# Lone attention with two key chunks per tile and other small vector operations, and the first rank mix placed among batch 1's heads

## The chip, the cores and the metric

The kernel runs on one core of a Trainium2 chip. The metric is the device time of one execution in microseconds (us), as a median over runs. The engines are named as the profile does: PE is TensorE (PEld its weight loads), DVE is VectorE, ACT is ScalarE, POOL is GpSimd, and SP is SyncE, which issues nearly all DMAs here. Each engine works through its own queue of instructions in order. The source is written against a framework that fixes each engine's order when the kernel is built, with a timing model of its own; the order in which the source names things sets priorities, and only DMAs marked for it keep the source's order.

## The reference

Four batches of 448 tokens go through attention with 12 heads of 64, then through two mixers. All weights arrive as float64, and the kernel rebuilds float32 values from their bits.

```python
q_n, k_n = rmsnorm(q, g_q), rmsnorm(k, g_k)      # over the 64 of a head, eps 1e-6
attn = softmax(q_n @ k_n.T / 8)                  # sum + 1e-9
x = (attn @ v) as (B, S, 768)
# first mixer: rank 32 over the tokens, then 768 -> 3072 -> 768
u = x + (x.T @ U @ V).T
x = u + relu(u @ w_ch1) @ w_ch2
# second mixer: 448 -> 256 -> 448 over the tokens, then 768 -> 1536 -> 768
u = x + (relu(x.T @ w_tok1) @ w_tok2).T
out = u + relu(u @ w_ch1) @ w_ch2
```

## The kernel before, in words

Tokens are split into NC4 = 4 chunks of CP = 112. Most products run in float32r on a value split in a high part (ACT copy) and a low part (DVE or POOL subtraction), so that one float32 product becomes two or three.

**Attention** goes by pairs of heads. `load_pair` (L187) loads q, k, v, squares q on ACT (L204) and k with `mul` (L202; POOL's tensor_mul, DVE's for the very first pair), sums on DVE (L205), and forms 1/rms with small operations on 16 columns: L206 (mean and eps), Ln and Exp on ACT (L208, L209), one Newton step on DVE (L211 to L214). `turn_pair` (L233) transposes q and k on PE and rebuilds them, with DMAs on SP, as operands of a split product. `softmax` (L267) makes for each query chunk the scores in PSUM (`sc`), their negated maximum on DVE (L276), the exp on ACT (L278); after each second chunk DVE makes 1/(sum + 1e-9) (L281, L282) and POOL scales p (L285). `weigh` (L288) does for each key chunk `kc`: four PE transposes of p into a PSUM tile `pt` (L304), a copy to `ph` on ACT (L312), the rest `pl` on DVE (L316), and the products with v into `pv`. One head of each pair of batches 0 and 1 is `whole`: its products stay float32 (no `pl`). At the end `pv` goes into `xT` (L321, or L324 and L325).

`attention` (L327) is a generator: at step t it runs the softmax of head t + 1 beside the weighing of head t, chunk by chunk, turns the pair two ahead and loads the pair four ahead. Batches 0 and 1 (24 heads) run alone in the loop at L563; at step 8 U and V are loaded there (`load_uv`, L161). The loop breaks after t = 23. Then the first two w1 chunks are loaded, the PSUM and SBUF pools are closed and opened anew (L573 to L577), and the rank mix of batches 0 and 1 follows (L578). From L595 on, attention of batches 2 and 3 runs beside the first feed-forward layer of batches 0 and 1.

**Rank mix** (`rank_mix`, L392) does for each half of the channels: PE transposes back to tokens (`pt_x`, L372) with high and low parts on ACT (L379) and DVE (L380), products with U into `ps_h`, their copy `hst` (L404, L405), products with V into `ps_u`, and `split_u` (L384): DVE adds into xT (L385), ACT (L386) and POOL (L387) make `u`.

**Feed-forward** (`ffn`, L447) takes chunks of 128 hidden channels in groups of G = 2: `first` multiplies with a w1 chunk (`ps_g`, `gs`), `second` with a w2 chunk (`ps_x`) and adds to xT (L478). A weight chunk is loaded by `to_f32` (L111) into one of two raw buffers, rebuilt by ACT (L123, L128), DVE (L124, L125, L129) and POOL (L132), and split (L142 on ACT, L143 on POOL) into a destination from `slots` (L135), of which there are four high and four low. U takes one such pair of slots and V another, until the rank mixes have read them.

PSUM has eight banks. In lone attention: `s` (scores) three, `t` one, `p` four, and `pv` comes from `p` too. After the seam: `p` two, `v` one, `s` two, `t` one, `m` two.

Of the kernel before, what the change touches and what calls it, by code (L numbers as in the profile page):

```python
# [9 lines left out]
F32 = mybir.dt.float32  # L10
# [14 lines left out]
def attention_then_two_mixers(  # L25
# [28 lines left out]
    nc = tc.nc  # L54
# [8 lines left out]
    RC = T // P  # L63
    HALF = DM // 2
    G = 2
    PAIRS = ((0, 1), (2, 3))

    const = ctx.enter_context(tc.tile_pool(name="const", bufs=1))
    wp = ctx.enter_context(tc.tile_pool(name="wp", bufs=1))
# [19 lines left out]
    nc.vector.tensor_mul(gg, gq2, gk2)  # L89
    nc.vector.tensor_scalar_mul(gg, gg, 1.0 / D ** 0.5)  # L90

    def cols(x):
        return x.rearrange("r (c p) -> r c p", c=NC4)

# [1 line left out]
        return x.rearrange("r (p c) -> r c p", c=NC4)  # L96

    pools = {"late": False}
    AT = dict(qr=2, kr=2, vr=3, qn=1, vs=2, p=8, ph=3, pl=3, sq=1)

    def open_pools(stack, side):
        for nm, bufs, space in side:
# [84 lines left out]
    def load_pair(b, hp, whole, mul):  # L187
        h0 = 2 * hp
        raw = []
        for nm, src in (("q", q), ("k", k), ("v", v)):  # L190
            t = pools["at"].tile([CP, 2, NC4, D], F32, tag=f"{nm}r", bufs=AT[nm + "r"],
                        name=f"{nm}r")
            nc.sync.dma_start(t, src[b, h0:h0 + 2].rearrange("h (p c) d -> p h c d", c=NC4))
            raw.append(t)
        qr, kr, vr = raw

        ms = pools["at"].tile([CP, 2, 8], F32, tag="ms", name="ms")
        for i, t in enumerate((qr, kr)):
            sq = pools["at"].tile([CP, 2 * NC4, D], F32, tag="sq", bufs=AT["sq"], name="sq")
            tt = t.rearrange("p h c d -> p (h c) d")  # L200
            if i:
                mul(sq, tt, tt)  # L202
            else:
                nc.scalar.activation(sq, tt, AF.Square)  # L204
            nc.vector.reduce_sum(ms[:, i], sq, axis=AX.X)  # L205
        nc.vector.tensor_scalar(ms, ms, 1.0 / D, 1e-6, op0=ALU.mult, op1=ALU.add)  # L206
        rs = pools["at"].tile([CP, 2, 8], F32, tag="rs", name="rs")
        nc.scalar.activation(rs, ms, AF.Ln)  # L208
        nc.scalar.activation(rs, rs, AF.Exp, scale=-0.5)  # L209
        nt = pools["at"].tile([CP, 2, 8], F32, tag="nt", name="nt")  # L210
        nc.vector.tensor_mul(nt, rs, rs)  # L211
        nc.vector.tensor_mul(nt, nt, ms)
        nc.vector.tensor_scalar(nt, nt, -0.5, 1.5, op0=ALU.mult, op1=ALU.add)
        nc.vector.tensor_mul(rs, rs, nt)  # L214

        def scale(i, shape):
            return rs[:, i].rearrange("p (h c) -> p h c", h=2).unsqueeze(3).to_broadcast(shape)

        qn, kn = [], []
        for i, (nm, t, n) in enumerate((("qn", qr, qn), ("kn", kr, kn))):  # L220
            n.append(pools["at"].tile([CP, NC4, 2, D], F32, tag=nm, bufs=AT["qn"], name=nm))
            mul(
                n[0].rearrange("p c h d -> p h c d"), t, scale(i, [CP, 2, NC4, D]))
        qn, kn = qn[0], kn[0]

        vs = pools["at"].tile([CP, 2, NC4, 2, D], F32R, tag="vs", bufs=AT["vs"], name="vs")
        js = [j for j in range(2) if j not in whole]
        if js:
            js = slice(js[0], js[-1] + 1)
            split(vr[:, js], vs[:, js, :, 0], vs[:, js, :, 1])  # L230
        return qn, kn, [vr[:, j] if j in whole else vs[:, j] for j in range(2)]
# [35 lines left out]
    def softmax(pr, qs, ks, kt):  # L267
        for c in range(NC4):
            if c % 2 == 0:
                sm = pools["at"].tile([CP, 2], F32, tag="sm", bufs=6, name="sm")  # L270
            sc = psum("s", [CP, S], "sc")
            cs = slice(c * CP, (c + 1) * CP)
            mm(sc, qs[:, cs], ks, True, False)
            mm(sc, qs[:, cs], kt, False, True)
            nm = pools["at"].tile([CP, 1], F32, tag="nm", bufs=8, name="nm")
            nc.vector.tensor_reduce(nm, sc, axis=AX.X, op=ALU.max, negate=True)  # L276
            p = pools["pp"].tile([CP, S], F32, tag="p", bufs=AT["p"], name="p")
            nc.scalar.activation(p, sc, AF.Exp, bias=nm, accum_out=sm[:, c % 2:c % 2 + 1])  # L278
            pr.append(p)
            if c % 2:  # L280
                nc.vector.tensor_scalar_add(sm, sm, 1e-9)  # L281
                nc.vector.reciprocal(sm, sm)  # L282
                for i in range(2):
                    x = pr[c - 1 + i]
                    nc.gpsimd.tensor_scalar(x, x, sm[:, i:i + 1], 1.0, op0=ALU.mult, op1=ALU.mult)  # L285
            yield

    def weigh(pr, vj, j, dst, whole):  # L288

        pv = psum("v", [P, S], "pv")  # L290

        def product(kc, ph, pl):
            if whole:
                mm(pv[:D], vj[:, kc], ph, kc == 0, kc == NC4 - 1)
                return
            vk = vj[:, kc].rearrange("p t d -> p (t d)")
            mm(pv, vk, ph, kc == 0, False)
            mm(pv, vk, pl, False, kc == NC4 - 1)

        last = None  # L300
        for kc in range(NC4):
            pt = psum("p", [CP, S], "pt")
            for c in range(NC4):
                nc.tensor.transpose(  # L304
                    pt[:, c * CP:(c + 1) * CP], pr[c][:, kc * CP:(kc + 1) * CP],
                    ident[:CP, :CP],
                )
            if last:
                product(*last)
            ph = pools["pp"].tile([CP, S], F32 if whole else F32R, tag="ph", bufs=AT["ph"],  # L310
                                  name="ph")
            nc.scalar.activation(ph, pt, AF.Copy)  # L312
            pl = None
            if not whole:
                pl = pools["pp"].tile([CP, S], F32R, tag="pl", bufs=AT["pl"], name="pl")
                nc.vector.tensor_sub(pl, pt, f(ph))  # L316
            last = kc, ph, pl
            yield
        product(*last)
        if whole:  # L320
            nc.vector.tensor_copy(dst[j * D:(j + 1) * D], pv[:D])  # L321
            return
        tmp = pools["at"].tile([D, S], F32, tag="tmp", bufs=1, name="tmp")
        nc.scalar.activation(tmp, pv[D:], AF.Copy)  # L324
        nc.vector.tensor_add(dst[j * D:(j + 1) * D], pv[:D], tmp)  # L325
# [39 lines left out]


    def to_tokens(xT, hf):
        row = []
        for c in range(NC4):
            pt = psum("p", [CP, HALF], "pt_x")  # L370
            for i in range(3):
                nc.tensor.transpose(  # L372
                    pt[:, i * P:(i + 1) * P],
                    xT[:, 3 * hf + i, c * CP:(c + 1) * CP], ident,
                )
            s = (pools["xs"].tile([CP, 2, HALF], F32R, tag="xs", name="xs") if pools["xs"] is not pools["g"]
                 else pools["g"].tile([P, 2, S], F32R, tag="g", name="xs")[:CP, :, :HALF])
            hi, lo = s[:, 0], s[:, 1]
            nc.scalar.activation(hi, pt, AF.Copy)  # L379
            nc.vector.tensor_sub(lo, pt, f(hi))  # L380
            row.append((hi, lo))
        return row

    def split_u(xT, cc, pu, u):  # L384
        nc.vector.tensor_add(xT[:, cc], pu, xT[:, cc])  # L385
# [6 lines left out]
    def rank_mix(xT, uv):  # L392
# [1 line left out]
        u4, vh, vl = uv  # L394
        u = new_u()
        for hf in range(2):
            xs = to_tokens(xT, hf)
            ph = psum("t", [P, HALF], "ps_h")
            for c in range(NC4):
                for i in range(2):  # L400
                    mm(ph, u4[:, c].rearrange("p t r -> p (t r)"), xs[c][i],
                       c == 0 and i == 0, c == NC4 - 1 and i == 1)
            hst = pools["hs"].tile([P, HALF], F32R, tag="hs", name="hst")
            nc.scalar.activation(hst, ph, AF.Copy)  # L404
# [9 lines left out]
    def token_mix(xT, w):  # L414

        u = new_u()
        for hf in range(2):
            xs = to_tokens(xT, hf)
            ts = []
            for rc in range(RC):  # L420
                pt = psum("t", [P, HALF], "ps_t1")
# [124 lines left out]
    with ExitStack() as stack:  # L546
        open_pools(stack, (("hs", 1, 0), ("at", 2, 0)))
        inner = stack.enter_context(ExitStack())
        AT.update(p=12, ph=4, pl=4)
        open_pools(inner, (("pp", 1, 0), ("s", 3, 1), ("t", 1, 1), ("p", 4, 1)))  # L550
        pools["v"] = pools["p"]

        def new_xo():
            return pools["at"].tile([P, S], F32, tag="xo", bufs=1, name="xo")
# [8 lines left out]
        for t in att:  # L563
            if t == 8:
                pools["late"] = True
                uv = load_uv(False)
                pools["late"] = False
            if t == 2 * H - 1:
                break
        pools["late"] = True  # L570
        w1s = [w1_chunk(wa1, j) for j in range(G)]
        pools["late"] = False
        inner.close()  # L573
        AT.update(p=8, ph=3, pl=3)
        open_pools(stack, (("pp", 1, 0), ("g", 2 * G + 1, 0), ("p", 2, 1), ("v", 1, 1),
                           ("s", 2, 1), ("t", 1, 1), ("m", 2, 1)))
        pools["xs"] = pools["g"]  # L577
        for i in range(2):  # L578
            us[i] = rank_mix(xs[i], uv)


        def mix(i):
# [2 lines left out]
        def swap():  # L585
            for _ in att:
# [2 lines left out]
            open_pools(rest, (("wt", 1, 0), ("g", 2 * G, 0), ("xs", 8, 0), ("hs", 2, 0),  # L589
                              ("ts", 4, 0), ("ot", 2, 0), ("x3", 1, 0),  # L590
                              ("m", 3, 1), ("s", 2, 1), ("t", 1, 1), ("p", 2, 1)))
            wt.extend(load_wt())
            kept.extend(load_uv(True))

# [56 lines left out]
```

## Time and profile before

| | us |
|---|---|
| median of 3 runs | 1592.1 (1589.14 to 1592.72) |
| profiled execution, its own time | 1583.41 |
| profiled execution, span from first to last instruction | 1581.6 |
| lone attention, first score to last product | about 21 to 200.6 |
| seam with both rank mixes | about 200 to 241 |
| attention of batches 2 and 3 beside the first feed-forward layer | about 240 to 610 |

A row of the profile by line gives: line, engine, operation, out<-in with shapes and count, then busy time in us and mean ns of one, then the idle time just before and what ended it. A row of the timeline gives start, length, engine, line, operation and, in brackets, the idle time before it with its releaser. Spans are counted from the first instruction.

### The profile page before, as it was taken

How to read it: one execution, taken by the hardware profiler on the slowest of the kernel's cores; microseconds unless marked ns; L12 is line 12 of the kernel's file. 1: busy time of each engine (PE TensorE's matmuls, PEld its weight loads, DVE VectorE, ACT ScalarE, POOL GpSimd, SP SyncE). 2: the span in 40 equal slices, each digit the busy share in tenths (PEclk: the TensorE clock that was granted, in tenths of full speed). 3: DMA queues.
4: the chain of work that ended last, by engine and by line, in shares of the span. 5: the costliest groups of instructions: out<-in, count | busy, mean ns of one | idle time of the engine just before them, and what ended most of it. 6: DMA issues, size and time to landing. Idle time of an engine off the chain costs nothing.

```text
span 1581.6 us, 21878 instructions
## 1 busy us (share of the span) xinstructions
PE 1496.0 (95%) x7648; PEld 1303.0 (82%) x7648; DVE 1192.7 (75%) x1981; ACT 815.7 (52%) x1511; POOL 847.2 (54%) x645
## 2 busy tenths in 40 slices
PE   5999978999999999999999999999999999999998
PEld 3565566888788899898898988889999998998997
DVE  6899888988897887667858677677676676748663
ACT  5888765666566665434534345344344343524431
POOL 4667656666666554544745454455455453535540
PEclk9999979999999999999999999999999999999999
DMA  6656533445434422323314334233333332203312
GB/s 154 155 154 165 149 130 113 127 130 157 144 112 139 116 92 83 122 91 113 120 43 137 101 100 150 66 116 133 101 101 120 100 110 90 80 13 120 128 61 71
DMA packets 116046, 178.22 MB, mean 113 GB/s; under 512 B 9248, under 2 KB 105984, under 8 KB 115936
## 3 DMA queue, kind: packets, MB, share of 16 engines
q1 hardware_dynamic: 115616, 176.82, 36.7%
q8 instruction: 61, 1.00, 0.3%
q14 instruction: 49, 0.40, 0.1%
q10 hardware_dynamic: 320, 0.00, 0.0%
HBM read 135.50 MB, written 8.26 MB: 91 GB/s over the span
## 4 chain that ended last, share of the span: by engine, by line
PE 62%; DVE 12%; POOL 4%; DMA 4%; ACT 3%; issue 2%; SPq 0%; DVEq 0%; POOLq 0%; ACTq 0%
PE ps_x L77 27%; PE ps_g L77 25%; DVE w_bits L124 3%; DVE w_bits L129 2%; PE ps_u L77 2%; PE ps_t L77 2%; POOL w L143 2%; PE pv L77 2%; DMA qs<-hi 2%; DMA w_raw<-in_moe_w_ch_dram 1%; POOL w_bits L132 1%; DVE w_bits L125 1%; PE sc L77 1%; PE pt L304 1%; DVE xT L478 1%
## 5 line engine op out<-in xcount | busy, mean ns | idle before, releaser
L77 PE MATMUL ps_x<-gs,w 128*128 128x448 f32 x2592 | 566.5, 370 | 22.1 <-DVE xT L478 11.5
L77 PE MATMUL ps_g<-u,w 128*128 128x448 f32 x2592 | 546.4, 367 | 1.6 <-DVE gs L465 0.9
L77 PEld LDWEIGHTS ps_x<-gs,w 128*128 128x128 f32 x2592 | 483.4, 190 | 71.5 <-DVE xT L478 18.0
L77 PEld LDWEIGHTS ps_g<-u,w 128*128 128x128 f32 x2592 | 484.1, 188 | 42.2 <-DVE gs L465 1.5
L132 POOL TENSOR_TENSOR w_bits<-w_bits,w_round 128x768 uint32<-128x768 uint32 (+2 forms) x152 | 279.8, 1841 | 270.7 <-DVE w_bits L129 211.9
L143 POOL TENSOR_TENSOR w<-w_bits,w 128x768 fp32r<-128x768 f32 (+3 forms) x154 | 285.9, 1866 | 199.2 <-ACT w L142 198.9
L478 DVE TENSOR_TENSOR xT<-ps_x,xT 128x448 f32<-128x448 f32 x432 | 265.9, 619 | 121.4 <-PE ps_x L77 119.6
L128 ACT ACTIVATE w_round<-w_raw 128x768 uint32<-128x768 uint32 (+2 forms) x152 | 135.2, 889 | 186.2 <-POOL w_bits L132 186.0
L124 DVE TENSOR_SCALAR w_bits<-w_bits 128x768 f32<-128x768 f32 (+2 forms) x152 | 145.3, 956 | 96.0 <-ACT w_bits L123 95.9
L142 ACT ACTIVATE w<-w_bits 128x768 fp32r<-128x768 f32 (+3 forms) x154 | 124.8, 830 | 124.0 <-PE ps_x L77 68.0
L285 POOL TENSOR_SCALAR p<-p,sm 112x448 f32<-112x448 f32 x192 | 129.0, 685 | 95.3 <-DVE sm L282 49.0
L123 ACT ACTIVATE w_bits<-w_raw 128x768 f32<-128x768 f32 (+2 forms) x152 | 135.3, 891 | 85.5 <-POOL w L143 77.7
L129 DVE SCALAR_TENSOR_TENSOR w_bits<-w_raw,w_bits 128x768 uint32<-128x768 uint32 (+2 forms) x152 | 168.7, 1110 | 2.1
L278 ACT ACTIVATE p<-sc,nm 112x448 f32<-112x448 f32 x192 | 121.9, 637 | 49.8 <-DVE nm L276 41.9
L125 DVE TENSOR_SCALAR w_bits<-w_bits 128x768 uint32<-128x768 uint32 (+2 forms) x152 | 137.7, 906 | 2.9
L464 ACT ACTIVATE gs<-ps_g 128x448 fp32r<-128x448 f32 x144 | 77.8, 543 | 108.8 <-PE ps_g L77 106.1
L465 DVE SCALAR_TENSOR_TENSOR gs<-ps_g,gs 128x448 fp32r<-128x448 f32 x144 | 88.9, 619 | 52.8 <-ACT gs L464 52.5
L276 DVE TENSOR_REDUCE nm<-sc 112x1 f32<-112x448 f32 x192 | 116.3, 613 | 8.4 <-PE sc L77 7.8
L304 PEld LDWEIGHTS pt<-ident,p 112*112 112x112 f32 x768 | 86.7, 134 | 41.5 <-issue 18.5
L312 ACT ACTIVATE ph<-pt 112x448 fp32r<-112x448 f32 (+1 forms) x192 | 101.3, 546 | 30.2 <-PE pt L304 29.0
L304 PE MATMUL pt<-ident,p 112*112 112x112 f32 x768 | 111.4, 262 | 5.2 <-DVE pl L316 2.6
L387 POOL TENSOR_TENSOR u<-xT,u 128x448 fp32r<-128x448 f32 x48 | 59.1, 1248 | 65.5 <-ACT u L386 65.5
(74 smaller groups left out, 1438.4 us busy)
## 6 DMA issues: line engine op xcount, KB each, us to landing
w_raw<-in_moe_w_ch_dram SPq DMA_DIRECT2D x144, 768.0 KB, 4.4
ks<-hi SPq DMA_DIRECT2D x96, 112.0 KB, 2.4
kt<-lo SPq DMA_DIRECT2D x96, 112.0 KB, 2.3
qr<-in_q_dram SPq DMA_DIRECT2D x24, 224.0 KB, 3.1
kr<-in_k_dram SPq DMA_DIRECT2D x24, 224.0 KB, 3.2
vr<-in_v_dram SPq DMA_DIRECT2D x24, 224.0 KB, 3.1
qs<-hi SPq DMA_DIRECT2D x48, 112.0 KB, 2.8
qs<-lo SPq DMA_DIRECT2D x48, 112.0 KB, 2.7
```

The source lines that it names most:

```text
L77: nc.tensor.matmul(o, lhsT=l, rhs=r, start=start, stop=stop)
L123: nc.scalar.activation(f(w), f(high), AF.Abs)
L124: nc.vector.tensor_scalar_max(f(w), f(w), TINY)
L125: nc.vector.tensor_scalar(w, w, 3, 0x3FFFFFF8, op0=ALU.logical_shift_left, op1=ALU.bitwise_and)
L128: nc.scalar.activation(r, low, AF.Copy, scale=2.0 ** -29)
L129: nc.vector.scalar_tensor_tensor(w, high, 0xC0000000, w, op0=ALU.bitwise_and, op1=ALU.bitwise_or)
L132: nc.gpsimd.tensor_tensor(w, w, r, op=ALU.add)
L142: nc.scalar.activation(hi, w, AF.Copy)
L143: nc.gpsimd.tensor_sub(lo, w, f(hi))
L285: nc.gpsimd.tensor_scalar(x, x, sm[:, i:i + 1], 1.0, op0=ALU.mult, op1=ALU.mult)
L304: nc.tensor.transpose(pt[:, c * CP:(c + 1) * CP], pr[c][:, kc * CP:(kc + 1) * CP], ident[:CP, :CP],)
L478: nc.vector.tensor_add(xT[:, dc], px, xT[:, dc])
```

## The change

- In lone attention `weigh` takes two key chunks per tile (`AT["turn"]` = 2): `pt` becomes a tile of two banks, with one ACT copy and one DVE subtraction over both chunks. Later attention keeps one chunk per tile.
- PSUM in lone attention: `s` two banks, `t` one, `p` two tiles of two banks, `pv` one bank of its own. `ph` and `pl` have two buffers of double size.
- The square of q uses `mul` (POOL, or DVE for the first pair), as that of k, in all attention.
- Four kinds of small DVE operation on 2 or 16 columns become scalar_tensor_tensor, two of them with a constant tile (`eps`, `zeros`) as second input; the Newton step has three operations in place of four.
- `rank_mix` of batch 0 is called at step t = 13 of the loop of lone attention, with its `xs` tiles in the buffers of `ph`. `rank_mix` of batch 1 stays behind the loop. `to_tokens` is a generator.

```diff
-    AT = dict(qr=2, kr=2, vr=3, qn=1, vs=2, p=8, ph=3, pl=3, sq=1)
+    AT = dict(qr=2, kr=2, vr=3, qn=1, vs=2, p=8, ph=3, pl=3, sq=1, turn=1)
...
-            if i:
-                mul(sq, tt, tt)
-            else:
-                nc.scalar.activation(sq, tt, AF.Square)
+            mul(sq, tt, tt)
             nc.vector.reduce_sum(ms[:, i], sq, axis=AX.X)
-        nc.vector.tensor_scalar(ms, ms, 1.0 / D, 1e-6, op0=ALU.mult, op1=ALU.add)
+        nc.vector.scalar_tensor_tensor(
+            ms, ms, 1.0 / D, eps[:CP], op0=ALU.mult, op1=ALU.add)
...
-        nc.vector.tensor_mul(nt, rs, rs)
+        nc.vector.scalar_tensor_tensor(nt, rs, -0.5, rs, op0=ALU.mult, op1=ALU.mult)
         nc.vector.tensor_mul(nt, nt, ms)
-        nc.vector.tensor_scalar(nt, nt, -0.5, 1.5, op0=ALU.mult, op1=ALU.add)
-        nc.vector.tensor_mul(rs, rs, nt)
+        nc.vector.scalar_tensor_tensor(rs, nt, 1.5, rs, op0=ALU.add, op1=ALU.mult)
...
-                nc.vector.tensor_scalar_add(sm, sm, 1e-9)
+                nc.vector.scalar_tensor_tensor(
+                    sm, sm, 1e-9, zeros[:CP], op0=ALU.add, op1=ALU.add)
...
-        for kc in range(NC4):
-            pt = psum("p", [CP, S], "pt")
-            for c in range(NC4):
-                nc.tensor.transpose(
-                    pt[:, c * CP:(c + 1) * CP], pr[c][:, kc * CP:(kc + 1) * CP],
-                    ident[:CP, :CP],
-                )
+        n = AT["turn"]
+        for k0 in range(0, NC4, n):
+            kcs = range(k0, k0 + n)
+            pt = psum("p", [CP, n, BANK], "pt")[:, :, :S]
+            for i, kc in enumerate(kcs):
+                for c in range(NC4):
+                    nc.tensor.transpose(
+                        pt[:, i, c * CP:(c + 1) * CP], pr[c][:, kc * CP:(kc + 1) * CP],
+                        ident[:CP, :CP],
+                    )
             if last:
                 product(*last)
...
-                pl = pools["pp"].tile([CP, S], F32R, tag="pl", bufs=AT["pl"], name="pl")
+                pl = pools["pp"].tile([CP, n, S], F32R, tag="pl", bufs=AT["pl"], name="pl")
                 nc.vector.tensor_sub(pl, pt, f(ph))
-            last = kc, ph, pl
-            yield
+            last = kcs, ph, pl
+            for _ in kcs:
+                yield
...
-        AT.update(p=12, ph=4, pl=4)
-        open_pools(inner, (("pp", 1, 0), ("s", 3, 1), ("t", 1, 1), ("p", 4, 1)))
-        pools["v"] = pools["p"]
+        AT.update(p=12, ph=2, pl=2, turn=2)
+        open_pools(inner, (("pp", 1, 0), ("s", 2, 1), ("t", 1, 1), ("p", 2, 1), ("v", 1, 1)))
...
+            if t == H + 1:
+                pools["new_xs"] = lambda: pools["pp"].tile(
+                    [CP, 2, S], F32R, tag="ph", bufs=AT["ph"], name="xs")
+                us[0] = rank_mix(xs[0], uv)
             if t == 2 * H - 1:
                 break
...
-        for i in range(2):
-            us[i] = rank_mix(xs[i], uv)
+        pools["new_xs"] = lambda: pools["g"].tile([P, 2, S], F32R, tag="g", name="xs")
+        us[1] = rank_mix(xs[1], uv)
```

## Rows read from the trace of the kernel before

**Rows 1.** Busy time of the engines, share of the span, instructions.
```profile
PE 1496.0 (95%) x7648; PEld 1303.0 (82%) x7648; DVE 1192.7 (75%) x1981; ACT 815.7 (52%) x1511; POOL 847.2 (54%) x645
```

**Rows 2.** Stages: length, busy of each engine (instructions), PE's granted clock, DMA share, GB/s.
```profile
25.00:200.00 175.00, 164.09 (x862) 101.67 (x861) 157.44 (x389) 142.48 (x381) 112.32 (x151) 0.99 0.63 160
200.00:241.00 41.00, 33.12 (x150) 27.70 (x149) 32.96 (x49) 27.16 (x49) 26.28 (x18) 0.79 0.32 105
241.00:248.00 7.00, 0.77 (x5) 0.32 (x3) 7.00 (x4) 1.67 (x5) 5.22 (x5) 0.86 0.12 33
```

**Rows 3.** Timeline of the seam, engine by engine: start, length, instruction, idle before.
```profile
200.18 0.47 PE L77 MATMUL pv<-pl,vs 112*128 112x448 f32 x1
...
203.75 0.69 PE L77 MATMUL ps_h<-xs,w 112*128 112x384 f32 x1 [3.10 <-ACT xs L379]
...
237.12 0.68 PE L77 MATMUL ps_x<-gs,w 128*128 128x448 f32 x2 [1.41 <-ACT w L142]
...
239.63 0.62 DVE L385 TENSOR_TENSOR xT<-ps_u,xT 128x448 f32<-128x448 f32 x1 [0.24 <-PE ps_u L77]
240.31 6.32 DVE L124 TENSOR_SCALAR w_bits<-w_bits 128x768 f32<-128x768 f32 x1
...
236.20 0.86 ACT L142 ACTIVATE w<-w_bits 128x768 fp32r<-128x768 f32 x1
...
216.61 1.83 POOL L132 TENSOR_TENSOR w_bits<-w_bits,w_round 128x768 uint32<-128x768 uint32 x1 [0.96 <-DVE w_bits L129]
```

**Rows 4.** Rank mixes: pieces of the chain (start, length), then groups from 188 to 241.
```profile
221.85 1.24 PE ps_g L77 x6
...
223.89 0.35 PE ps_h L77 x2
...
225.65 0.33 PE pt_x L372 x3
...
232.34 0.83 PE ps_u L77 x4
...
L387 POOL TENSOR_TENSOR u<-xT,u 128x448 fp32r<-128x448 f32 x9 | 10.8, 1223 | 5.4 <-ACT u L386 5.4
...
L380 DVE TENSOR_TENSOR xs<-pt_x,xs 112x384 fp32r<-112x384 f32 x16 | 8.5, 551 | 2.7 <-ACT xs L379 2.5
...
L385 DVE TENSOR_TENSOR xT<-ps_u,xT 128x448 f32<-128x448 f32 x12 | 7.1, 617 | 2.7 <-PE ps_u L77 2.7
```

**Rows 5.** Groups by line and shape in lone attention, 25 to 200 us.
```profile
L276 DVE TENSOR_REDUCE nm<-sc 112x1 f32<-112x448 f32 x93 | 56.1, 613 | 3.8 <-PE sc L77 3.5
...
L205 DVE TENSOR_REDUCE ms<-sq 112x8 f32<-112x512 f32 x28 | 18.8, 673 | 2.8 <-POOL sq L202 1.6 <-ACT sq L204 1.2
...
L202 POOL TENSOR_TENSOR sq<-kr 112x512 f32<-112x512 f32 x14 | 14.7, 1050 | 6.9 <-DMA kr<-in_k_dram 3.3 <-DVE ms L205 1.5 <-DVE sm L281 1.4
```

**Rows 6.** Small operations: duration min/median/max in ns over the run; one stall's timeline.
```profile
L206 DVE TENSOR_SCALAR ms<-ms x24: 148/172/4299, 8.9 to 456.7; 112x16 f32<-112x16 f32 x24
...
L213 DVE TENSOR_SCALAR nt<-nt x24: 148/175/3693, 12.0 to 461.5; 112x16 f32<-112x16 f32 x24
...
L214 DVE TENSOR_TENSOR rs<-rs,nt x24: 148/174/1740, 12.2 to 463.1; 112x16 f32<-112x16 f32 x24
...
273.25 3.69 DVE L213 TENSOR_SCALAR nt<-nt 112x16 f32<-112x16 f32 x1
...
273.29 1.84 POOL L132 TENSOR_TENSOR w_bits<-w_bits,w_round 128x768 uint32<-128x768 uint32 x1
275.09 1.82 POOL L143 TENSOR_TENSOR w<-w_bits,w 128x768 fp32r<-128x768 f32 x1
...
278.53 0.59 PE L304 MATMUL pt<-ident,p 112*112 112x112 f32 x4 [2.62 <-DVE pl L316]
```

**Rows 7.** The scores `sc` from 25 to 200 us: one group, one wait (us, times).
```profile
L278 ACT ACTIVATE p<-sc,nm x94: 617/635/694, 25.3 to 187.1; 112x448 f32<-112x448 f32 x94
...
  ACT p L278: 9.6, 21
```

More of the change, by code (lines that the diff above doesn't have):

```diff
@@ L65, in attention_then_two_mixers @@
     G = 2
-    PAIRS = ((0, 1), (2, 3))
+    BANK = 512
     const = ctx.enter_context(tc.tile_pool(name="const", bufs=1))
@@ L90, in attention_then_two_mixers @@
     nc.vector.tensor_scalar_mul(gg, gg, 1.0 / D ** 0.5)
+    zeros = const.tile([P, 2], F32, name="zeros")
+    nc.vector.memset(zeros, 0.0)
+    eps = const.tile([P, 16], F32, name="eps")
+    nc.vector.memset(eps, 1e-6)
     def cols(x):
@@ L200, in load_pair @@
             tt = t.rearrange("p h c d -> p (h c) d")
-            if i:
-                mul(sq, tt, tt)
-            else:
-                nc.scalar.activation(sq, tt, AF.Square)
+            mul(sq, tt, tt)
             nc.vector.reduce_sum(ms[:, i], sq, axis=AX.X)
-        nc.vector.tensor_scalar(ms, ms, 1.0 / D, 1e-6, op0=ALU.mult, op1=ALU.add)
-        rs = pools["at"].tile([CP, 2, 8], F32, tag="rs", name="rs")
+        ms = ms.rearrange("p a b -> p (a b)")
+        nc.vector.scalar_tensor_tensor(
+            ms, ms, 1.0 / D, eps[:CP], op0=ALU.mult, op1=ALU.add)
+        rs = pools["at"].tile([CP, 16], F32, tag="rs", name="rs")
         nc.scalar.activation(rs, ms, AF.Ln)
         nc.scalar.activation(rs, rs, AF.Exp, scale=-0.5)
-        nt = pools["at"].tile([CP, 2, 8], F32, tag="nt", name="nt")
-        nc.vector.tensor_mul(nt, rs, rs)
+        nt = pools["at"].tile([CP, 16], F32, tag="nt", name="nt")
+        nc.vector.scalar_tensor_tensor(nt, rs, -0.5, rs, op0=ALU.mult, op1=ALU.mult)
         nc.vector.tensor_mul(nt, nt, ms)
-        nc.vector.tensor_scalar(nt, nt, -0.5, 1.5, op0=ALU.mult, op1=ALU.add)
-        nc.vector.tensor_mul(rs, rs, nt)
+        nc.vector.scalar_tensor_tensor(rs, nt, 1.5, rs, op0=ALU.add, op1=ALU.mult)
+        rs = rs.rearrange("p (a b) -> p a b", a=2)
         def scale(i, shape):
@@ L290, in weigh, with product @@
         pv = psum("v", [P, S], "pv")
[L292 to L298, printed above, removed]
-        last = None
-        for kc in range(NC4):
-            pt = psum("p", [CP, S], "pt")
-            for c in range(NC4):
-                nc.tensor.transpose(
-                    pt[:, c * CP:(c + 1) * CP], pr[c][:, kc * CP:(kc + 1) * CP],
-                    ident[:CP, :CP],
-                )
+        def product(kcs, ph, pl):
+            for i, kc in enumerate(kcs):
+                if whole:
+                    mm(pv[:D], vj[:, kc], ph[:, i], kc == 0, kc == NC4 - 1)
+                    continue
+                vk = vj[:, kc].rearrange("p t d -> p (t d)")
+                mm(pv, vk, ph[:, i], kc == 0, False)
+                mm(pv, vk, pl[:, i], False, kc == NC4 - 1)
+        last = None
+        n = AT["turn"]
+        for k0 in range(0, NC4, n):
+            kcs = range(k0, k0 + n)
+            pt = psum("p", [CP, n, BANK], "pt")[:, :, :S]
+            for i, kc in enumerate(kcs):
+                for c in range(NC4):
[3 more added lines that the diff above has]
+                    )
             if last:
                 product(*last)
-            ph = pools["pp"].tile([CP, S], F32 if whole else F32R, tag="ph", bufs=AT["ph"],
+            ph = pools["pp"].tile([CP, n, S], F32 if whole else F32R, tag="ph", bufs=AT["ph"],
                                   name="ph")
@@ L367, in to_tokens @@
     def to_tokens(xT, hf):
-        row = []
         for c in range(NC4):
@@ L375, in to_tokens @@
                 )
-            s = (pools["xs"].tile([CP, 2, HALF], F32R, tag="xs", name="xs") if pools["xs"] is not pools["g"]
-                 else pools["g"].tile([P, 2, S], F32R, tag="g", name="xs")[:CP, :, :HALF])
+            s = pools["new_xs"]()[:CP, :, :HALF]
             hi, lo = s[:, 0], s[:, 1]
@@ L380, in to_tokens @@
             nc.vector.tensor_sub(lo, pt, f(hi))
-            row.append((hi, lo))
-        return row
+            yield hi, lo
     def split_u(xT, cc, pu, u):
@@ L396, in rank_mix @@
         for hf in range(2):
-            xs = to_tokens(xT, hf)
             ph = psum("t", [P, HALF], "ps_h")
-            for c in range(NC4):
+            for c, xs in enumerate(to_tokens(xT, hf)):
                 for i in range(2):
-                    mm(ph, u4[:, c].rearrange("p t r -> p (t r)"), xs[c][i],
+                    mm(ph, u4[:, c].rearrange("p t r -> p (t r)"), xs[i],
                        c == 0 and i == 0, c == NC4 - 1 and i == 1)
@@ L417, in token_mix @@
         for hf in range(2):
-            xs = to_tokens(xT, hf)
+            xs = list(to_tokens(xT, hf))
             ts = []
@@ L573, in attention_then_two_mixers @@
         inner.close()
-        AT.update(p=8, ph=3, pl=3)
+        AT.update(p=8, ph=3, pl=3, turn=1)
         open_pools(stack, (("pp", 1, 0), ("g", 2 * G + 1, 0), ("p", 2, 1), ("v", 1, 1),
                            ("s", 2, 1), ("t", 1, 1), ("m", 2, 1)))
-        pools["xs"] = pools["g"]
-        for i in range(2):
-            us[i] = rank_mix(xs[i], uv)
+        pools["new_xs"] = lambda: pools["g"].tile([P, 2, S], F32R, tag="g", name="xs")
+        us[1] = rank_mix(xs[1], uv)
         def mix(i):
@@ L591, in swap @@
                               ("m", 3, 1), ("s", 2, 1), ("t", 1, 1), ("p", 2, 1)))
+            pools["new_xs"] = lambda: pools["xs"].tile([P, 2, HALF], F32R, tag="xs", name="xs")
             wt.extend(load_wt())
```

## The prediction

> **What bounds the kernel now.** I read the page's busy line first: TensorE is busy 95% of the span, VectorE 75% [rows 1]. So only time in which TensorE is kept waiting can be won. The table by stage tells where that is [rows 2]. From 460 us on (the pure feed-forward layers) nothing is touched. From 25 to 200 us attention of batches 0 and 1 runs alone: TensorE 164.09 of 175 us (94%) and VectorE 157.44 (90%), so two engines are near full there and work added to either costs about its own length. From 200 to 241 us, the seam between lone attention and the first feed-forward layer, TensorE shows 33.12 of 41 us, part of it at a granted clock of 0.79 on average (below the 2.4 GHz level); and from 241 to 248 us it does 0.77 of 7 us.
>
> The timeline of the seam shows why [rows 3]. The last product of lone attention starts at 200.18; the first rank-mix product at 203.75; the last addition of the two rank mixes is at 239.63. The first ps_x product, with which the second half of the first feed-forward group begins, is at 237.12 and waited for ACT's split of a w2 chunk (L142, 236.20). Those integer weights were ready at 216.61 + 1.83 = 218.4 us. What held the split was its destination: `slots()` has four buffers, U and V hold two until both rank mixes are over, and the two w1 chunks hold the others. So the path through the seam is: end of attention, rank mix 0, rank mix 1, U's slots free, w2 split, ps_x.
>
> **The change part by part.** 1. *Batch 0's rank mix leaves the seam.* The two mixes take 203.75 to 240.25 = 36.5 us, 18 us each, paced by the ACT, VectorE, TensorE relay and the weight chain between. With one left, U comes free some 18 us sooner. Batch 0's `u` exists already, so its ps_g products (36 in [rows 2]'s second stage, at a pure step of about 0.205 us, 1.24 us for six [rows 4], 7.4 us) can run beside mix 1 (7.9 us of TensorE, below): 15.3 of 18 us, so TensorE has room. Next late is the w2 chunk itself: ready 18 us after the end of attention (200.6 to 218.4), just when mix 1 would end (3 + 18 = 21 us after). So the weights take the rest of the gain at most in part: I take -16 us. Bounds: -18 if the mix is the only limit; -8 if the weight chain (four chunks through ACT, VectorE, POOL and two raw buffers) sets the pace.
>
> 2. *The same mix among batch 1's heads.* It issues no DMA; load_uv stays at t = 8, so SP's queue is not crossed. TensorE pieces at full clock [rows 4]: eight groups of three transposes at 0.33 us, 2.6; sixteen ps_h at 0.35 for two, 2.8; twelve ps_u at 0.83 for four, 2.5: 7.9 us. VectorE: 8 x 0.551 + 6 x 0.617 + 2 x 0.56 (two hst subtractions, taken as long as an xs one) = 9.2 us. POOL: six u subtractions at 1.223, 7.3 us, ahead of the p products (L285) that the transposes wait for. At 94% and 90% busy I charge +8 us. Bounds: +3 if the 11 us that TensorE lacks to 175 take half of it, +13 if VectorE's 9.2 us and the sharing of `ph`'s two buffers (xs uses them, and the heads' ph waits behind) add up.
>
> 3. *Two key chunks per tile.* One VectorE subtraction of 896 columns in place of two. L205 with 512 columns takes 673 ns, L276 with 448 takes 613 [rows 5]: 60 ns for 64 columns, so some 0.19 us of each instruction is fixed. Part of it overlaps with the neighbours; 24 merged pairs save at most 4.6 us of VectorE. ACT saves a like amount on 48 pairs, and the squares. TensorE saves nothing. As TensorE is as full as VectorE, I take -2 us (0 to -5).
>
> 4. *Square of q on POOL* in place of ACT: 24 x 1.05 us [rows 5], 12.6 of them in the 175 us where POOL is busy 112.32 [rows 2]. What waits behind it are the p products. Cover: POOL's idle third. +1 us (0 to +4). Head 0's square goes to VectorE, 0.69 us at most at the start, in these bounds.
>
> 5. *Other forms of the small operations.* VectorE's tensor_scalar on 16 columns (L206, L213) has a median of 172 to 175 ns, but maxima of 4.30 and 3.69 us; the two-tensor form L214, as small, stays at 1.74 at most [rows 6]. The long one at 273.25 ends as POOL's second instruction in a row (273.29, 275.09) does: a tensor_scalar waited through a hand-over between POOL instructions. The two-input forms waited too, but for one instruction (the longest there is 1.84 us). So scalar_tensor_tensor with a tile as second input should cap the wait at one POOL instruction, not remove it: of 3.69 + 4.30 us at most 1.84 each would be left, so 4.3 us or more of VectorE goes. TensorE lost 2.62 us at the first [rows 6]. I take -3 us (0 to -7), and the small operation that goes is in it.
>
> By the Trainium skill, page "SBUF — State Buffer", section "Who interferes with whom", a VectorE instruction with two SBUF inputs contends with a GpSimd instruction that reads SBUF just as a two-port mode does, and the second to start blocks fully. By that rule alone part 5 is 0 and the sum 3 us higher. The trace agrees that both forms wait; it does not show them waiting equally long.
>
> 6. *PSUM is dealt anew*: scores get two banks for three, pt two double banks, pv one bank of its own. This adds waits: with three banks score products already waited 21 times for exp, 9.6 us [rows 7]. Behind a waiting score on TensorE's queue stand transposes and products of the current head. Also pv of a head now waits for the last one's L325. +2 us; bounds 0 (pt's four chunks cover it) and +15 (next section).
>
> 7. *The 6.32 us wait of L124* at 240.31 [rows 3], which empties TensorE from 241 to 248, keeps its form. POOL's queue of u subtractions and splits ahead of it is halved, so it may go (-6) or come back elsewhere (0); I take 0.
>
> Sum: -16 + 8 - 2 + 1 - 3 + 2 + 0 = -10 us. The profiled execution took 1583.4 us (span 1581.6); it would come to about 1573. The median of the three timed runs is 1592.1, 0.55% above it, so I put the difference on the median: 1582.
>
> **The rivals.** A. *The score ring of two becomes the bound of lone attention (slower).* From starts and ends of the 94 scores of that stage [rows 7], a bank is held 3.7 us from product to end of exp on average, so three banks hold 1.96 at a time; with two there is no slack. 70 of 94 products began within 0.2 us of, or before, the end of the exp two chunks earlier, by 67 us in all. Against it: the holding time is mostly queueing (0.4 us product, 0.53 reduction, 0.55 exp, under 2 us with hand-overs) and shrinks when fewer are in flight. If a fifth of the 67 us comes back as waiting on TensorE, that is 13 us where I took 2: the sum is +1, and a third of it, 22 us, gives +10. It decides from 12 us, 0.5 us a head. Time 1593 to 1602.
>
> B. *The weights set the pace of the seam.* Then part 1 is -8 and the sum -2: 1590. For it: four chunks pass at about 6 us each (POOL's L132 of the third at 216.61). Against it: w2's chunk stood ready for 18 us.
>
> C. *The mix hides in lone attention and the L124 wait goes*: +3 and -6, giving -21: 1571.
>
> D. *The new forms change nothing* (both wait one POOL instruction or several alike): sum -7, 1585. The page named above states this rule.
>
> **How the numbers follow.** Two tenths of a per cent, 3.2 us, is about what a measurement of this kernel can tell from no change. Chances: forecast 0.40 (own range 1577 to 1588), D 0.10, C 0.13, B 0.15, A 0.22. Faster by over 0.2%: forecast, D, C and a little of B, 0.65. Same: most of B and the mild end of A, 0.14. Slower: the rest of A and of B, 0.21. The range goes from C's 1571 to within A, 1598, leaving out under 2 in 10.
>
> **What would show it.** Right: the last addition of the rank mix (L385) some 18 us after the end of lone attention, not 39; first ps_x about 20 us after it, not 36.5; lone attention ending 5 to 9 us later; no small scalar_tensor_tensor over 2 us. Wrong: waits of sc for exp in lone attention well over 9.6 us (A); the split L142 of w2 waiting for POOL's L132 and not for the rank mix (B); L281, L206 at 4 us again (D).

## The result and the profile after

The changed kernel took 1603.83 us (median of four runs, 1602.32 to 1605.74) against 1590.8 us before (median of four runs, the three known before and one more): ratio 1.0082, 95% interval 1.0062 to 1.0102. It is 13 us slower where 10 us faster was forecast. The profiled execution took 1602.33 us, its span 1600.5 us. That is 18.9 us more than the profiled execution of before, whose 1583.41 us lie under all of its timed runs; differences between stages, below, are between profiled executions.

The busy line, then the stages of the changed kernel (columns as in [rows 1] and [rows 2]): lone attention, the seam, and the stretch of lone attention that holds batch 0's rank mix.

```profile
PE 1501.5 (94%) x7648; PEld 1310.9 (82%) x7648; DVE 1192.5 (75%) x1936; ACT 798.9 (50%) x1439; POOL 870.1 (54%) x668
...
25.00:235.00 210.00, 180.27 (x910) 113.90 (x909) 164.69 (x361) 138.57 (x333) 130.33 (x169) 0.98 0.53 132
235.00:266.00 31.00, 21.33 (x94) 18.20 (x94) 24.34 (x34) 18.81 (x33) 20.09 (x13) 0.78 0.35 115
142.00:160.00 18.00, 15.91 (x82) 10.74 (x82) 11.42 (x25) 10.88 (x24) 7.35 (x8) 1.00 0.16 36
```

The engines' work is about what it was. Lone attention is 35 us longer (210 us where [rows 2] had 175), and its two busiest engines are further from full: TensorE 86%, VectorE 78%. The seam is shorter. So in lone attention engines wait for one another more than before. The timeline of the seam, engine by engine, as in [rows 3]:

```profile
234.78 0.37 PE L77 MATMUL pv<-pl,vs 112*128 112x448 f32 x1
238.47 0.69 PE L77 MATMUL ps_h<-xs,w 112*128 112x384 f32 x1 [3.32 <-ACT xs L388]
242.96 1.01 PE L77 MATMUL ps_h<-xs,w 112*128 112x384 f32 x2 [3.81 <-DVE xs L389]
...
247.19 3.65 PE L77 MATMUL ps_g<-u,w 128*128 128x448 f32 x16
...
251.64 3.96 PE L77 MATMUL ps_g<-u,w 128*128 128x448 f32 x18
...
259.34 1.04 PE L77 MATMUL ps_h<-xs,w 112*128 112x384 f32 x2 [1.12 <-ACT xs L388]
...
263.94 0.96 PE L77 MATMUL ps_x<-gs,w 128*128 128x448 f32 x2
...
238.19 3.00 DVE L218 SCALAR_TENSOR_TENSOR rs<-nt,rs 112x16 f32<-112x16 f32 x1
...
242.35 1.02 DVE L389 TENSOR_TENSOR xs<-pt_x,xs 112x384 fp32r<-112x384 f32 x2
...
265.61 0.61 DVE L393 TENSOR_TENSOR xT<-ps_u,xT 128x448 f32<-128x448 f32 x1
...
260.86 0.87 ACT L147 ACTIVATE w<-w_bits 128x768 fp32r<-128x768 f32 x1
...
237.41 1.99 POOL L148 TENSOR_TENSOR vs<-vr,vs 112x512 fp32r<-112x512 f32 x1 [8.00 <-ACT vs L147]
239.37 1.79 POOL L137 TENSOR_TENSOR w_bits<-w_bits,w_round 128x768 uint32<-128x768 uint32 x1
...
251.80 1.86 POOL L137 TENSOR_TENSOR w_bits<-w_bits,w_round 128x768 uint32<-128x768 uint32 x1 [0.96 <-DVE w_bits L134]
```

Lone attention ends at 235.15 (234.78 + 0.37), not 200.65: +34.5 us. From there to the first ps_x is 28.8 us, not 36.5: -7.7 us. That is 26.8 us in all; some 8 us of it are won back later, beside the attention of batches 2 and 3. The scores' waits, counted as in [rows 7], from 25 to 236 us (us, times):

```profile
  ACT p L283: 42.7, 67
```

[rows 7] had 9.6 us in 21 waits. That is the sign that the prediction named for rival A.

### The profile page after: what moved, and what is told of

Read it like the earlier page. It is cut to its first block, busy times and chain, and to the rows that moved or that the text cites. A ratio compares the mean times of both kernels' runs of the same rounds, so it can differ in the third digit from the quotient of the medians.

```text
span 1600.5 us, 21731 instructions
## 1 busy us (share of the span) xinstructions
PE 1501.5 (94%) x7648; PEld 1310.9 (82%) x7648; DVE 1192.5 (75%) x1936; ACT 798.9 (50%) x1439; POOL 870.1 (54%) x668
## 4 chain that ended last, share of the span: by engine, by line
PE 67%; DVE 16%; POOL 5%; ACT 5%; DMA 3%; issue 3%; SPq 1%; ACTq 0%; DVEq 0%; POOLq 0%
PE ps_x L77 27%; PE ps_g L77 24%; PE pv L77 4%; PE sc L77 3%; PE pt L314 3%; DVE w_bits L134 3%; DVE w_bits L129 2%; POOL w_bits L137 2%; POOL w L148 2%; PE ps_u L77 2%; PE ps_t L77 2%; DVE nm L281 1%; DVE w_bits L130 1%; DVE xT L485 1%; DVE pl L326 1%
## 5 line engine op out<-in xcount | busy, mean ns | idle before, releaser
L129 DVE TENSOR_SCALAR w_bits<-w_bits 128x768 f32<-128x768 f32 (+2 forms) x152 | 138.0, 908 | 93.6 <-ACT w_bits L128 93.4
L134 DVE SCALAR_TENSOR_TENSOR w_bits<-w_raw,w_bits 128x768 uint32<-128x768 uint32 (+2 forms) x152 | 163.4, 1075 | 2.4
L130 DVE TENSOR_SCALAR w_bits<-w_bits 128x768 uint32<-128x768 uint32 (+2 forms) x152 | 144.1, 948 | 2.9
L322 ACT ACTIVATE ph<-pt 112x448 fp32r<-112x448 f32 (+2 forms) x144 | 93.7, 668 | 43.6 <-PE pt L314 43.1
L77 PE MATMUL sc<-ks,qs 128*112 128x448 f32 x192 | 83.6, 437 | 28.7 <-ACT p L283 23.1
```

Of the source, the lines that this page charges most:

```text
L77: nc.tensor.matmul(o, lhsT=l, rhs=r, start=start, stop=stop)
L129: nc.vector.tensor_scalar_max(f(w), f(w), TINY)
L130: nc.vector.tensor_scalar(w, w, 3, 0x3FFFFFF8, op0=ALU.logical_shift_left, op1=ALU.bitwise_and)
L134: nc.vector.scalar_tensor_tensor(w, high, 0xC0000000, w, op0=ALU.bitwise_and, op1=ALU.bitwise_or)
```

## The experiments

Times are medians; a difference in us is the ratio's excess times 1590. "Lone attention ends" is the end of its last product with v.

**One part at a time: the PSUM deal.** `e1_sc2`, `e10_ring2` and `e9_pvbank` change one line of the kernel before:

```diff
-        open_pools(inner, (("pp", 1, 0), ("s", 3, 1), ("t", 1, 1), ("p", 4, 1)))
-        pools["v"] = pools["p"]
+ e1_sc2:     ("s", 2, 1), ("t", 1, 1), ("p", 4, 1), ("v", 1, 1)
+ e10_ring2:  ("s", 2, 1), ("t", 1, 1), ("p", 5, 1);  pools["v"] = pools["p"]
+ e9_pvbank:  ("s", 3, 1), ("t", 1, 1), ("p", 3, 1), ("v", 1, 1)
```

> The kernel before with one edit in lone attention's PSUM: scores two banks for three, pv one bank of its own, pt four banks. Nothing else. Theory R (the score ring of two sets the cadence of lone attention): scores wait for exp some 35 to 45 us in all against 9.6, the last product of lone attention ends 12 to 22 us later than at 200.6, time 1600 to 1612. Rival V (the double tile, the forms or POOL's squares set it): within 4 us of before.

> The kernel before with two banks for scores and five for pt and pv together. Theory R: lone attention ends 18 to 28 us later, 1608 to 1618, scores wait for exp 30 us or more. Rival P: within 6 us of before.

> The kernel before with pv in one bank of its own, scores three and pt three banks. Theory R: within 6 us of before (lone attention ends within 6 us of 200.6); the loss of e1_sc2 (26 us) comes from the scores' third bank. Rival P (the one bank of pv, which waits for the evacuation L324, L325, is the loss): 1605 or more.

Measured: `e1_sc2` 1615.7 us (ratio 1.0164, 1.0149 to 1.0179), +26 us, more than expected; `e10_ring2` 1611.8 (1.0147, 1.0114 to 1.0180), +23; `e9_pvbank` 1589.7 (0.9999, 0.9982 to 1.0017), level. For each, in this order, the wait of scores for exp in lone attention (us, times) and the last product:

```profile
  ACT p L278: 34.6, 53
...
226.24 0.47 PE L77 MATMUL pv<-pl,vs 112*128 112x448 f32 x1
```
```profile
  ACT p L278: 45.6, 62
...
220.93 0.47 PE L77 MATMUL pv<-pl,vs 112*128 112x448 f32 x1 [0.72 <-DVE pl L316]
```
```profile
  ACT p L278: 20.8, 26
...
202.52 0.47 PE L77 MATMUL pv<-pl,vs 112*128 112x448 f32 x1
```

Two banks for scores alone cost lone attention 21 to 26 us, with or without a bank of its own for pv; that bank alone costs nothing. In `e9_pvbank` the same waits doubled and the time stayed, so their sum is a sign and not the price. The price shows in the rate: the 96 scores began one each 1.73 us before, and one each 2.06 and 1.96 us in the two kernels with two banks, which is 31 and 22 us for 96. From the start of a score's first product to the end of its exp, a bank was held 3.62 us on average before, and 3.12 and 3.05 us in those two. The hold divided by the time from one score to the next gives the banks in use: 2.1 of three before, 1.5 of two. That the hold alone doesn't set the rate is shown by `e15_order_kq` below: it has three banks and a hold of 3.04 us, and its scores come one each 1.79 us.

`e17_ring4` gives a fourth bank to the scores: `("s", 4, 1), ("t", 1, 1), ("p", 3, 1)`, pv from `p`.

> The kernel before with four banks for scores and three for pt and pv together. Theory R with a hold of about 3.1 us or more whatever the ring: three banks (hold 3.7 us, a chunk each 1.74 us, 2.1 in use) are already enough, waits of scores for exp fall under 5 us, time within 11 us of before, which is what order by itself is worth. If scores still set the pace at three: 12 us or more faster. If pt and pv in three banks become short: 12 us or more slower.

Measured: 1604.4 us (1.0091, 1.0060 to 1.0123), +14. The waits of scores for exp, counted as in [rows 7], had been expected to fall under 5 us; they rose from 9.6 to 17.1 us. Pt and pv had become short of banks, as the waits of TensorE's loads for ACT's copy of pt show. First before (25 to 200 us; us, times, longest), then `e17_ring4` (25 to 217 us):

```profile
PEld sc L77 <- ACT p L278: 7.2, 15, 0.8
PEld pv L77 <- DVE pl L316: 3.7, 6, 0.9
PEld pv L77 <- ACT ph L312: 6.1, 11, 1.0
PEld pt L304 <- ACT ph L312: 0.3, 2, 0.2
```
```profile
PEld sc L77 <- ACT p L278: 12.3, 23, 2.2
PEld pv L77 <- DVE pl L316: 9.4, 19, 1.1
PEld pv L77 <- ACT ph L312: 9.2, 17, 2.0
PEld pt L304 <- ACT ph L312: 8.0, 9, 1.8
```

A score was then held 5.11 us, 2.34 of them between the end of the reduction and the start of exp (0.88 before). The fourth bank let scores run ahead, and exp came no sooner. No deal that was tried beat three and four.

**The change without the early mix, and without the double tile.** `e2_nomix` takes the call of `rank_mix` at t = 13 out of the changed kernel and runs both mixes in the seam. `e8_nomix_turn1` takes the double tile out as well:

```diff
-        AT.update(p=12, ph=2, pl=2, turn=2)
-        ... ("s", 2, 1), ("t", 1, 1), ("p", 2, 1), ("v", 1, 1)
+        AT.update(p=12, ph=4, pl=4)
+        ... ("s", 2, 1), ("t", 1, 1), ("p", 4, 1), ("v", 1, 1)
```

> The changed kernel, but with batch 0's rank mix back in the seam ahead of batch 1's. Theories R and V (attention's own cadence is lost, about 20 us, whatever stands in it): lone attention ends near 220, the seam is as long as before, time 1600 to 1612. Rival M (the mix among the heads is the whole loss): lone attention ends near 200, time within 4 us of before.

> The changed kernel without the early mix and with one key chunk per tile (pt four single banks, scores still two, pv one of its own): against e2_nomix it takes the double tile away alone. If the double tile saves what merging 24 subtractions can (2 to 5 us): 2 to 5 us slower than 1610.3. If it costs (coarser hand-overs): faster than 1607. If forms and squares win 8.7 us beside a ring of two as well, it is near 1615.7 - 8.7 = 1607.

Measured: `e2_nomix` 1610.3 us (1.0127, 1.0109 to 1.0145), lone attention ends at 219.5, its scores wait 38.7 us; `e8_nomix_turn1` 1620.5 us (1.0183, 1.0142 to 1.0223), it ends at 229.9, 44.2 us. So the loss is there without the early mix, which rules out rival M. Of the 34.5 us by which lone attention grew in the changed kernel, 18.8 stand without the early mix (219.5 against 200.65), and 15.7 come with it. Beside two score banks the kernel with the double tile was 9 us faster than that without, more than the 2 to 5 us expected; whether by the tile's work or by its order is taken up below.

**The early mix.** `e4_mixonly` adds it to the kernel before; `e3_turn1` is the changed kernel with the PSUM of before and one chunk per tile; `e13_forms_mix` is that with the squares back on ACT. In all three the mix has xs buffers of its own:

```diff
+            if t == H + 1:
+                pools["new_xs"] = lambda: pools["pp"].tile(
+                    [CP, 2, S], F32R, tag="xs", bufs=2, name="xs")
+                us[0] = rank_mix(xs[0], uv)
```

> The kernel before with the early mix alone (after step 13, xs in two buffers of their own); squares, forms, tiles and PSUM as before. My prediction's parts 1 and 2: lone attention ends 8 us later, the seam is 16 us shorter, time 1580 to 1586. Theory M (the mix stops attention, 16 us for 8 us of work): lone attention ends 14 to 18 us later, time 1588 to 1596.

> The changed kernel with one key chunk per tile and the PSUM deal of before (scores three banks, pt and pv four together); xs of the early mix in two buffers of their own. Squares on POOL, the other forms and the early mix stay. Theory R, or V by the double tile: lone attention ends 8 to 18 us later than at 200.6, the seam is 11 to 16 us shorter, time 1578 to 1592. Rival (squares and forms are the loss): time 1598 or more.

> The kernel before with the other forms and the early mix (xs in two buffers of their own); squares on ACT, one chunk per tile, PSUM of before. If the parts add up (forms -12 from e5_forms, early mix +7 from e4_mixonly): 1583 to 1588. If the early mix gains once VectorE has less to wait for: under 1578. If what e5_forms won is an order that came out well: anywhere within 8 us of before, with no relation to the two.

Measured: 1596.3 us (1.0043, 1.0024 to 1.0063), 1590.5 us (1.0015, 0.9998 to 1.0032) and 1587.1 us (0.9977, 0.9961 to 0.9993). The last product of lone attention and the first ps_x of `e4_mixonly`, then of `e3_turn1`:

```profile
217.10 0.47 PE L77 MATMUL pv<-pl,vs 112*128 112x448 f32 x1
...
245.39 0.65 PE L77 MATMUL ps_x<-gs,w 128*128 128x448 f32 x2
```
```profile
208.39 0.47 PE L77 MATMUL pv<-pl,vs 112*128 112x448 f32 x1
...
237.23 0.66 PE L77 MATMUL ps_x<-gs,w 128*128 128x448 f32 x2
```

What the early mix does is read from four pairs that differ by it alone (and its xs buffers): from the end of the last product of lone attention, from there to the first ps_x, and from the ratios of the times.

| pair | lone attention | seam | whole |
|---|---|---|---|
| `e4_mixonly` against before | +16.9 us | 36.5 to 27.8: -8.7 | +7 |
| `e13_forms_mix` against `e5_forms` | +10.2 | 36.4 to 28.4: -7.9 | +9 |
| `e3_turn1` against `e7_forms_squares` | +7.3 | 41.1 to 28.4: -12.7 | +2 |
| changed kernel against `e2_nomix` | +15.7 | 41.3 to 28.8: -12.5 | -7 |

The seam is 8 to 13 us shorter and lone attention 7 to 17 us longer; in three pairs of four the price is higher than the gain.

`e3_turn1` also answers for the PSUM deal and the double tile together: without them, all else but the xs buffers as in the change, lone attention ends 26 us sooner than in the changed kernel (208.86 against 235.15) and the whole is 11 us faster.

**The score ring given back to the changed kernel.** `e11_after_ring3` opens `("s", 3, 1), ("p", 2, 1), ("v", 1, 1)` with `pools["t"] = pools["s"]`.

> The changed kernel with three banks for scores that tt and ps_h share (the bank of t goes to them); pt two double banks, pv one, all else as in the change. Theory R: much of the 37 us of lone attention comes back; it ends near 215, time 1585 to 1597. If sharing with tt makes the ring as short as two: 1600 to 1606.

Measured: 1597.9 us (1.0053, 1.0035 to 1.0071). Lone attention ends at 220.8, 14 us sooner than in the changed kernel, and its scores wait 25.5 us. It is between the two expectations' marks; that tt and ps_h in the same three banks restore the ring only in part is the likely reason, but was not tested apart. 14 us in the stage are 5 us in the whole.

**Small operations and squares.** `e5_forms` is the kernel before with all four other forms, `e6_squares` with q's squares on `mul`, `e7_forms_squares` with both, `e16_two_forms` with these two forms alone:

```diff
-        nc.vector.tensor_scalar(ms, ms, 1.0 / D, 1e-6, op0=ALU.mult, op1=ALU.add)
+        nc.vector.scalar_tensor_tensor(ms, ms, 1.0 / D, eps[:CP], op0=ALU.mult, op1=ALU.add)
...
-                nc.vector.tensor_scalar_add(sm, sm, 1e-9)
+                nc.vector.scalar_tensor_tensor(sm, sm, 1e-9, zeros[:CP], op0=ALU.add, op1=ALU.add)
```

> The kernel before with the other forms of the small operations alone (the two constant tiles included). Theory F (the forms cap the waits for POOL, and with the squares they won the 8.7 us of lone attention by which the early mix cost 8.3 with them and 17.0 without): lone attention ends 4 to 9 us before 200.6, time 1580 to 1587. Rival, the rule that a two-input operation waits for POOL just as well: within 3 us of before, no change in lone attention.

> The kernel before with the squares of q on POOL alone. Theory F: within 3 us of before. Rival Q (ACT's relief won the 8.7 us): lone attention ends 4 to 9 us earlier, time 1580 to 1587. My prediction's part 4 had +1 us.

> The kernel before with forms and squares, no early mix, PSUM and tiles as before. If their gain does not depend on the early mix: lone attention ends 6 to 10 us before 200.6, time 1580 to 1586. If they only made the early mix cheaper: within 3 us of before.

> The kernel before with two of the other forms alone, sm (with the zeros) and ms (with the eps); the Newton step keeps its four operations. If a scalar_tensor_tensor waits less for POOL than a tensor_scalar (my part 5): 3 to 12 us faster. If the two wait alike, as the rule has it: within 3 us of before, or off by what e14 and e15 show for order.

Measured: 1578.2 us (0.9922, 0.9900 to 0.9944); 1589.8 (1.0009, 0.9984 to 1.0033); 1590.6 (1.0004, 0.9985 to 1.0024); 1599.1 (1.0060, 1.0038 to 1.0081). The forms were 12 us faster alone, level with the squares, and two of them 10 us slower. No theory of a part's worth has these signs. Nor is the gain where the expectations put it: lone attention ends at 202.1 us in `e5_forms`, 202.6 in `e6_squares` and 201.5 in `e7_forms_squares`, no sooner than the 200.65 of before. What the forms were meant to cap is not capped either. In `e7_forms_squares` a two-tensor operation on 16 columns (min/median/max over the run, then the longest one and POOL beside it):

```profile
L217 DVE TENSOR_TENSOR nt<-nt,ms x24: 143/175/4621, 8.2 to 491.0; 112x16 f32<-112x16 f32 x24
...
352.02 4.62 DVE L217 TENSOR_TENSOR nt<-nt,ms 112x16 f32<-112x16 f32 x1
...
351.77 1.26 POOL L291 TENSOR_SCALAR p<-p,sm 112x448 f32<-112x448 f32 x2 [4.83 <-DVE sm L288]
352.99 3.62 POOL L148 TENSOR_TENSOR w<-w_bits,w 128x768 fp32r<-128x768 f32 x2
```

It waited through four POOL instructions to 356.6, longer than any tensor_scalar of [rows 6]. The scalar_tensor_tensor of ms in `e5_forms` has a maximum of 3.31 us, and in the changed kernel's seam, above, one of rs waited 3.00 us (238.19) until POOL's second instruction in a row ended:

```profile
L212 DVE SCALAR_TENSOR_TENSOR ms<-ms,eps x24: 157/257/3311, 9.0 to 468.4; 112x16 f32<-112x16 f32 x24
```

**What another order is worth.** `e12_control` adds the two constant tiles and nothing that reads them. `e14_order_p` and `e15_order_kq` change the order in which the source names two equal steps:

```diff
e14_order_p:
-                for i in range(2):
+                for i in (1, 0):
                     x = pr[c - 1 + i]
e15_order_kq:
-        for nm, src in (("q", q), ("k", k), ("v", v)):
+        for nm, src in (("k", k), ("q", q), ("v", v)):
```

> The kernel before with two constant tiles that are filled at the start and read by nobody: the order of the instructions, which is fixed when the kernel is built, may come out another way, and nothing else changes. If an order that differs by chance is worth little: within 3 us of before. If it is worth as much as e5_forms won: 6 to 14 us either way, and the gains of e5_forms and of the double tile can't be put down to their operations.

> The kernel before, with the two scalings of p that follow a reciprocal issued second first. The work is the same in number and form; the order fixed when the kernel is built comes out another way on every engine. If order by itself is worth little: within 3 us of before. If it is worth what e5_forms won: 5 us or more to either side.

> The kernel before with k loaded ahead of q; same work, another order on every engine. As for e14_order_p: within 3 us of before, or 5 us or more to either side.

Measured: `e12_control` 1588.1 us (0.9992, 0.9968 to 1.0016); but for the two fills it came out in the order of before on all engines, so it only shows that the tiles cost nothing. `e14_order_p` 1584.0 us (0.9969, 0.9957 to 0.9981), -5 us; `e15_order_kq` 1599.4 us (1.0064, 1.0045 to 1.0082), +10 us. Both do the same work in the same forms; the builder laid it out in another order on every engine. So in this kernel a difference of up to some 10 us between two sources can't be put down to the edit by a comparison of times alone; two such sources are few, and the spread may be wider. Beyond that spread are the four kernels with two score banks and whole seams, `e1_sc2`, `e10_ring2`, `e2_nomix` and `e8_nomix_turn1` (+20 to +29 us). The gain of `e5_forms` is barely beyond it.

## Why the prediction was wrong

**The step that failed is part 6, with rival A's price.** The sum had +2 us for the new deal of PSUM and a bound of +15; the score ring alone cost 23 to 26 us. Rival A named the mechanism, the place and the sign, and got 0.22. It was underpriced by one assumption: that the time a score's bank is held "is mostly queueing ... and shrinks when fewer are in flight", to under 2 us. It shrank from 3.62 to 3.1 us. The work itself takes 1.94 us of that: 0.69 from the start of a score's first product to the end of its second, 0.61 for the reduction, 0.64 for exp. (The prediction wrote 0.4, 0.53 and 0.55, though its own [rows 5] and [rows 7] have 613 and 635 ns for the last two.) What was left as queueing, between products and reduction and between reduction and exp, fell from 1.67 us to 1.14 and 1.13: by a third, and not to nearly nothing. The banks in use before were also 2.1 and not 1.96, because the 94 scores were spread over the whole 175 us, of which the last 12 have none.

The hold alone would still not have given the loss: two banks held 3.1 us each allow a chunk each 1.55 us, if both are always in use, against the 1.73 that were needed. But between the end of an exp and the start of the score that takes its bank the two kernels with two banks lost another 1.0 and 0.9 us on average, so only 1.5 banks were in use. In `e1_sc2` that is 93.8 us in all, and in 89.5 of them TensorE was busy with other work of its queue, nearly all of it transposes pt and products pv; only 40 of 94 scores began within 0.2 us of the release of their bank. So with two banks TensorE waits for exp at some scores and is late with its other work at the rest. Why this comes to 1.5 banks in use stays open.

**Part 1, the seam, was mis-sized.** -16 us were taken, and -8 to -13 measured in the four pairs; the last addition of the mix comes 31.1 us after the end of lone attention, where 18 were to be the sign. The path was right: the split of the w2 chunk (260.86) still follows the last ps_h (259.34 + 1.04 = 260.4), with its integers ready since 251.80 + 1.86 = 253.7. The error is "18 us each". The trace of before has the first mix's last addition here:

```profile
228.39 0.61 DVE L385 TENSOR_TENSOR xT<-ps_u,xT 128x448 f32<-128x448 f32 x1
```

That is 28.4 us after the end of lone attention; the second mix ended 11.2 us later, at 240.25. Six of its sixteen products with U had run by then, beside the first mix, so taking one mix away could win about 11 us and not 18. In the changed kernel TensorE works through 34 ps_g between the products of its one mix (sixteen from 247.19, eighteen from 251.64). The 3.81 us that it idles at 239 us, for a subtraction that came on VectorE's queue behind the small operation of 238.19, are not what keeps the seam long: `e4_mixonly` has no such wait and a seam of 27.8 us. What sets the pace of a mix alone stays open.

**Part 2 was too low in three pairs of four.** +8 us taken, bound 13; +7.3, +10.2, +15.7 and +16.9 measured. In the changed kernel the mix runs nearly as a block: no score is multiplied from 140.7 to 160.0 us, and from 142 to 160 us VectorE is busy only 11.42 of 18 us. That attention must then fill its pipe again is likely, and not shown. In the whole the early mix is worth between +9 and -7 us, which the spread of orders does not let one tell from nothing.

**Part 5 was wrong in its mechanism.** That a two-input form waits for one POOL instruction at most was read from 24 instances of each form and a difference of maxima. Rival D was right in its mechanism: all forms wait through several, and the changed kernel's scalar_tensor_tensor of 3.00 us is over the 2 us that the prediction named as its sign. By the Trainium skill (page "SBUF — State Buffer", section "Who interferes with whom") a VectorE instruction with two SBUF inputs contends with a GpSimd instruction that reads SBUF. The trace agrees, with the 4.62 us of `e7_forms_squares`, and adds that the wait can go on through four POOL instructions. Why `e5_forms` is 12 us faster stays open: its small operations waited as long (those over 0.3 us take 58.7 us in all, and 54.6 before), its order differs on every engine, and `e16_two_forms` went the other way.

**Parts 3 and 4.** The double tile came out better than -2 us beside two score banks (9 us by times). One subtraction over two chunks takes 1.08 us at the median, and one over a single chunk 0.61, so 24 merged pairs save 3.2 us of VectorE; the rest of the 9 is not explained. The squares came to +1 us alone (+1 taken) and +13 beside the forms. Both are within what order moves; neither is settled. **Part 7**: a stall of VectorE for POOL just behind the seam is still there in another instruction (L130, 4.81 us at 266.14), so 0 was right.

**The account.** Before to `e1_sc2` +26, with forms and squares (`e8_nomix_turn1`) +29, with the double tile (`e2_nomix`) +20, with the early mix (the changed kernel) +13. The first step is shown to be the ring: the four kernels with two score banks and whole seams lose 20 us or more, and the bank of pv alone loses nothing. The other three steps are each within the spread of orders.

The fastest version run is `e5_forms`, 1578.2 us, faster than both kernels by 12 and 25 us. It is the change with the forms alone.

## What to carry to other kernels

Before a bank is taken from a ring of PSUM tiles, work out from the trace how long each is held and how many are in use on average, and take the hold nearly as it stands: here the waiting in the queues of other engines shrank only by a third when fewer tiles were in flight. If banks divided by the hold comes near the rate that is needed, expect the ring to bound the stage: here two banks would have allowed a score each 1.55 us where 1.73 were needed, and gave 1.96 and 2.06. When a builder fixes the order, run one or two sources that differ in order alone, and believe no edit's gain that is smaller than their spread.

## What the runs showed that was not expected

A VectorE instruction on 16 columns that takes 0.175 us at the median waited 4.62 us while POOL went through four instructions without a pause; tensor_scalar and scalar_tensor_tensor waited through several too (longest in before 4.30 us, and in `e7_forms_squares` 4.19 us). And the order of the same instructions moved this kernel by -5 to +10 us.
